# Second-layer weight blocks decoded at other beats, GpSimd tied to row maxima through pair 10, and other beats for two preparation steps

## The chip, the cores and the metric

The kernel runs on one core of a Trainium2 chip. The metric is device time in microseconds (us), the median of several runs. The core's engines each take their own instructions in order: TensorE (PE, matmuls into PSUM), VectorE (DVE), ScalarE (ACT) and GpSimd (POOL). SyncE (SP) issues most DMAs.

## The reference

Eight batches of 12 heads, 448 rows, head size 64, all in float32. Queries and keys are normalised by their root mean square and a gain, softmax attention follows, and its output feeds a layer that takes the largest of three products.

```python
q_n, k_n = (rmsnorm(q, g_q), rmsnorm(k, g_k))
scores = scale * np.matmul(q_n, k_n.transpose(0, 1, 3, 2))
scores = scores - np.max(scores, axis=-1, keepdims=True)
attn = np.exp(scores)
attn = attn / (np.sum(attn, axis=-1, keepdims=True) + 1e-09)
attn_out = np.matmul(attn, v)
x = attn_out.transpose(0, 2, 1, 3).reshape(B * S, H * D)       # 3584 x 768
h = np.maximum(np.maximum(x @ w1, x @ w2), x @ w3)
out = h @ w_out
```

## The kernel before

**Pairs, chunks, beats.** Two heads of a batch make a pair g; there are 48 pairs, six to a batch. The 448 query rows of a pair go in four chunks c = 0 to 3, the last half as large. The whole order of work is written out by hand: the function `beat(g, i)` is called for each pair with i = 0 to 11, and every engine gets its instructions in the order in which the beats emit them. A counter `clock` counts beats (12 g + i), and `later(n, work)` emits work at the end of the beat n beats on. Chunk (g, c) below is chunk c of pair g.

**One chunk.** PE multiplies queries and keys into a PSUM tile `sc` (`scores`, L680, and L687 for the short chunk) at beat 12 g + 3 c - 1. There are two such tiles, so the scores of a chunk can start only when the chunk two earlier has let its tile go. DVE reads the tile for the row maximum (`row_max`, L702), from chunk (6, 1) on at the beat 12 g + 3 c, ACT takes the exponential (L718), DVE adds a small number to the sums and inverts them (L798, L802), ACT writes the upper float16 half of the weights `pp` (L805), and DVE writes the lower half from `sc` and `pp` (`lower_weights`, L815). That last instruction, one for each head, lets `sc` go; it is emitted right behind the row maximum of the next chunk. SP transposes `pp` by DMA (L828, L834) into `pt`, and PE multiplies it with the values (L860). The first six pairs (`PLAIN`) do this in float32 and transpose on PE (L738, copied out by ACT at L751).

**Preparing a pair.** Two pairs ahead, GpSimd squares the rows (L450), DVE sums them (L457), GpSimd forms the inverse root (L467, L471) and scales keys and queries (L479, L488). ACT writes their upper halves (L499), GpSimd the lower halves `kp` and `qp` (L505), and SP transposes both (L519) and swaps the keys' halves (L526). The values of a pair are scaled on GpSimd (L633), and split by ACT (L641) and GpSimd (L647). For the first three batches a bound on the values is found with products on PE (`largest_v`, L593: twelve matmuls into a PSUM tile `marks`) that DVE reduces (L169, `v_rows`); for later ones DVE reduces the values itself, in two parts.

**Weights.** The weights come as 24 blocks of 128 by 768, 18 of the first layer and six of the second, and each is decoded once. `prep_block(n)` has ACT rescale it (L189) and DVE run three steps on it, one to three beats apart (L197, L201, L206, 128x768 words each, SBUF to SBUF). A second-layer block is then multiplied with itself on PE (L260, six matmuls into `marks`, seven beats on) and reduced by DVE (L169, `o_row`, nine beats on). First-layer blocks are scaled and split in threes by ACT (L310) and DVE (L313). When the sixth second-layer block is decoded, `bound_out` starts ten beats on, and ACT (L365) and DVE (L370) split the six. `load_raw` brings the next raw block, by SP.

**The layer's matmuls.** `ffn` makes a queue of them for a batch, layer 1 (L889) and layer 2 (L951), and `thirds` lets some two groups of three out in each beat, between the attention's instructions. The queue opens at beat 78. All PSUM tiles but `sc` and the attention's output share one ring of three (`ps_m`): `acc` of the layer, `marks`, `most`, `turned`. What takes a tile of the ring waits until the tile three before it has been read.

**The tie.** `follow` (L164, L165) puts a 1x1 memset on DVE and a 1x1 copy of it on GpSimd, so that GpSimd goes on only when DVE has come that far. It stands ahead of every row maximum up to chunk (6, 0), and nowhere later. The lines that set the beats of the second-layer blocks are

```python
n_in = min(decoded[0], NFT * NJ)
due_at = BLOCK_BEATS[0] * n_in + BLOCK_BEATS[1] * (decoded[0] - n_in)
if decoded[0] < len(blocks) and clock[0] > due_at:
    later(0, lambda n=decoded[0]: prep_block(n), True)
```

with `BLOCK_BEATS = (4, 8)`: first-layer blocks at beats 1, 5, ... 69, second-layer blocks at 73, 81, 89, 97, 105, 113.

Of the kernel before, what the change touches and what calls it, by code (L numbers as in the profile page):

```python
# [32 lines left out]
SQUARE = 1.0 + 2.0 ** -5  # L33


BLOCK_BEATS = (4, 8)


PLAIN = 6


LOADS = 14
# [6 lines left out]
def qknorm_attention_maxout_ffn_kernel(  # L49
# [43 lines left out]
    NFT = DF // P  # L93
# [1000 lines left out]
    def beat(g, i):  # L1094
# [6 lines left out]
        if part == 0:  # L1101
            if g < G:
                if k > 4 * PLAIN:
                    row_max(g, c)
                softmax(g, c)
            if early:
                scores(*divmod(k + 1, 4))
            if g < PLAIN:
                if c > 0:
                    turn_plain(g, c - 1)  # L1110
            elif k == 4 * PLAIN:
                pass
            elif 0 < k <= 4 * G:
                lower_weights(*divmod(k - 1, 4))
# [32 lines left out]
        if g + 1 < G:  # L1147
            if g + 1 < PLAIN:
                if i in (1, 4):
                    turn_whole(g + 1, "kq"[i // 4])  # L1150
                if i in (2, 5):
                    keep_whole(g + 1, "kq"[i // 5])
            else:
                if i == 0:
                    upper_rows(g + 1, "q")
                if i in (0, 1):
                    lower_rows(g + 1, "kq"[i])
                if i in (2, 3):
                    turn_rows(g + 1, "kq"[i - 2])
                if i == 5:  # L1160
                    swap_keys(g + 1)

# [15 lines left out]
        elif n < G:  # L1178
            if i in (0, 3):
                squares(n, "kq"[i // 3])  # L1180
            if i in (2, 5):
                sum_squares(n, "kq"[i // 3])
            if i in (5, 7):
                inv_rms(n, "kq"[i // 7])
            if i in (8, 9):
                scale_rows(n, "kq"[i - 8])

        if g == 0 and i in (0, 3):
            load_v(i // 3)
            later(10 if i == 0 else 11, lambda: largest_v(i // 3))  # L1190
        if g % 3 == 0 and g + 6 < G and i == 9:
            load_v(g // 3 + 2)
            later(8, lambda: largest_v(g // 3 + 2))
        if g == 1 and i == 4:
            bound_v(0)
        if g % NP == NP - 1 and g + 1 < G and i == 7:
# [16 lines left out]
            turn_weights(w, 3)  # L1213
        if PLAIN <= g < G and i in (5, 8, 11):
            turn_weights(g, i // 3 - 1)
        n_in = min(decoded[0], NFT * NJ)
        due_at = BLOCK_BEATS[0] * n_in + BLOCK_BEATS[1] * (decoded[0] - n_in)
        if decoded[0] < len(blocks) and clock[0] > due_at:
            later(0, lambda n=decoded[0]: prep_block(n), True)
            decoded[0] += 1  # L1220
        tick()
# [41 lines left out]
```

## Time and profile before

| what | us |
|---|---|
| median of 3 runs | 1016.45 |
| range of the runs | 1015.76 to 1019.43 |
| the profiled execution's own time | 1017.41 |
| its span in the trace | 1015.6 |
| PE busy | 977.4 |
| DVE busy | 692.9 |
| ACT busy | 624.7 |
| GpSimd busy | 602.4 |

The span leaves 1.8 us outside the trace. A timeline row gives start, duration, engine, line, operation and tiles, and in brackets the idle time before it and what ended it. A row of windows gives for a stretch its length, the busy time of PE, PE's weight loads (PEld), DVE, ACT and GpSimd with the count of instructions, the granted PE clock as a share of full speed, the DMA engines' share and GB/s. "PE is busy" means that a matmul is in flight.

In the trace before, beat 73 lies near 111 us, beat 80 (scores of chunk (6, 3)) at 127.4, beat 83 (scores of (7, 0)) at 133.9 and beat 95 (scores of (8, 0)) at 158.3.

### The profile page before, as it was taken

The numbers are of one execution on the slowest core, as the hardware profiler recorded it, in microseconds if no ns is written. First come the engines' busy times: TensorE is split into PE (matmuls) and PEld (weight loads), VectorE is DVE, ScalarE is ACT, GpSimd is POOL, SyncE is SP. The second block draws the span as 40 slices with busy tenths as digits, with TensorE's granted clock in tenths as the row PEclk, the third lists the DMA queues.
The fourth block names the chain that finished last, engine by engine and source line by source line (L and its number), as shares of the span: only waits on it lengthen the run. The fifth ranks groups of instructions, "written<-read, shape, count | busy, mean of one in ns | idle before, by whom it ended". The sixth has DMA issues, their size and how long they took to land.

```text
span 1015.6 us, 17562 instructions
## 1 busy us (share of the span) xinstructions
PE 977.4 (96%) x6045; PEld 527.5 (52%) x6045; DVE 692.9 (68%) x1365; ACT 624.7 (62%) x1419; POOL 602.4 (59%) x683
## 2 busy tenths in 40 slices
PE   8988689889999999999999999999999999999998
PEld 5555345445555555555555555555555555555554
DVE  6899988887767666685767666775767657660120
ACT  6798675667666765666666666657666766651111
POOL 6677875678566666666776666666667757310000
PEclk9999889999999999999999999999999999999999
DMA  9867798989999899998989999999989998751001
GB/s 241 226 174 188 197 179 177 186 149 163 209 165 179 165 204 183 186 166 172 204 155 184 174 206 166 190 159 190 197 162 182 176 186 139 146 92 55 1 1 63
DMA packets 519550, 165.95 MB, mean 163 GB/s; under 512 B 494436, under 2 KB 515236, under 8 KB 519460
## 3 DMA queue, kind: packets, MB, share of 16 engines
q1 hardware_dynamic: 456480, 148.83, 75.5%
q10 hardware_dynamic: 62980, 16.00, 8.6%
q8 instruction: 48, 0.79, 0.3%
q14 instruction: 42, 0.34, 0.1%
HBM read 53.28 MB, written 11.01 MB: 63 GB/s over the span
## 4 chain that ended last, share of the span: by engine, by line
PE 60%; DMA 1%; DVE 0%; ACT 0%; issue 0%; SPq 0%
PE acc L889 34%; PE acc L951 12%; PE av L860 6%; PE sc L680 6%; PE sc L687 1%; DMA pt<-pp 0%; DVE pp L815 0%; DMA out_dram<-osb 0%; ACT osb L960 0%; DVE nm L702 0%; ACT pp L805 0%; ACT qp L499 0%; PE most L604 0%; ACT ht L909 0%; SPq L834 0%
## 5 line engine op out<-in xcount | busy, mean ns | idle before, releaser
L889 PE MATMUL acc<-xt,w_sb 128*128 128x448 f16 x2592 | 516.4, 354 | 0.0
L889 PEld LDWEIGHTS <-w_sb 128*128 128x128 f16 x2592 | 251.4, 98 | 242.3 <-issue 14.0
L718 ACT ACTIVATE sc<-sc,nm 128x448 f32<-128x448 f32 x294 | 178.9, 609 | 187.5 <-DVE nm L702 182.9
L702 DVE TENSOR_REDUCE nm<-sc 128x2 f32<-128x896 f32 x192 | 186.2, 970 | 99.4 <-PE sc L680 58.5
L805 ACT ACTIVATE pp<-sc,rs 128x448 f16<-128x448 f32 x294 | 173.0, 633 | 80.3 <-ACT sc L718 36.4
L815 DVE SCALAR_TENSOR_TENSOR pp<-sc,rs,pp 128x448 f16<-128x448 f32 x294 | 187.9, 675 | 0.9 <-ACT pp L805 0.9
L471 POOL TENSOR_TENSOR ri<-ri,half_neg 128x7 f32<-128x7 f32 x96 | 146.6, 1527 | 8.0
L951 PE MATMUL acc<-w_sb,ht 128*128 128x384 f16 x864 | 148.1, 326 | 1.6 <-ACT osb L960 1.3
L505 POOL TENSOR_TENSOR kp<-kn,kp 128x448 f16<-128x448 f32 x42 | 43.5, 1036 | 157.9 <-ACT kp L499 142.3
L680 PE MATMUL sc<-kt,qt 128*128 128x448 f16 x504 | 116.8, 354 | 10.6 <-DVE pp L815 10.4
L951 PEld LDWEIGHTS <-ht 128*128 128x128 f16 x864 | 83.7, 98 | 61.0 <-issue 5.8
L680 PEld LDWEIGHTS <-qt 128*128 128x128 f16 x504 | 48.8, 98 | 56.4 <-DVE pp L815 10.7
L860 PE MATMUL av<-pt,vp 128*64 128x448 f16 x672 | 72.6, 355 | 0.6 <-DMA pt<-pp 0.6
L918 POOL COPY hx<-ht 128x128 f16<-128x128 f16 x48 | 15.4, 322 | 95.6 <-DVE ht L913 94.9
L875 DVE SCALAR_TENSOR_TENSOR xt<-av,xt 128x448 f16<-128x448 f32 x42 | 26.2, 624 | 62.6 <-ACT xt L874 62.6
L647 POOL TENSOR_TENSOR vp<-vr,vp 128x512 f16<-128x512 f32 x42 | 49.3, 1174 | 21.0 <-ACT vp L641 21.0
L457 DVE TENSOR_REDUCE ss<-sq 128x7 f32<-128x448 f32 x96 | 57.9, 603 | 5.1 <-ACT sq L448 4.3
L505 POOL TENSOR_TENSOR qp<-qn,qp 128x448 f16<-128x448 f32 x42 | 46.3, 1103 | 22.3 <-ACT qp L499 21.4
L903 DVE TENSOR_TENSOR m<-acc,m 128x448 f32<-128x448 f32 x54 | 33.1, 614 | 33.1 <-PE acc L889 33.0
L860 PEld LDWEIGHTS <-vp 128*64 128x64 f16 x672 | 36.0, 109 | 34.7 <-issue 15.8
L488 POOL TENSOR_TENSOR qn<-qn,gain 128x448 f32<-128x448 f32 x42 | 49.0, 1167 | 3.3
L467 POOL TENSOR_SCALAR ri<-ss 128x7 f32<-128x7 f32 x54 | 20.1, 373 | 51.1 <-DVE ss L457 49.9
(140 smaller groups left out, 1159.2 us busy)
## 6 DMA issues: line engine op xcount, KB each, us to landing
raw<-in_moe_w_dram SPq DMA_DIRECT2D x18, 768.0 KB, 5.6
kt<-kt SPq DMA_DIRECT2D x84, 112.0 KB, 2.6
out_dram<-osb SPq DMA_DIRECT2D x24, 384.0 KB, 2.6
vr<-in_v_dram SPq DMA_DIRECT2D x42, 192.0 KB, 4.2
kr<-in_k_dram ACTq DMA_DIRECT2D x34, 224.0 KB, 3.1
qr<-in_q_dram ACTq DMA_DIRECT2D x34, 224.0 KB, 4.4
raw<-in_moe_w_out_dram SPq DMA_DIRECT2D x6, 768.0 KB, 5.0
vs<-vp SPq DMA_DIRECT2D x84, 48.0 KB, 2.5
```

The source lines that it names most:

```text
L457: nc.vector.tensor_reduce(sums[g % 2][:, KQ[what]], sq, axis=AX, op=ALU.add)
L471: nc.gpsimd.tensor_tensor(out=ri, in0=ri, in1=half_neg[:, at], op=ALU.pow)
L505: nc.gpsimd.tensor_tensor(out=parts[:, :, 1], in0=n, in1=parts[:, :, 0], op=ALU.subtract)
L647: nc.gpsimd.tensor_tensor(out=vp[:, 1], in0=values_of(g).rearrange("p h n d -> p (h n) d"), in1=vp[:, 0], op=ALU.subtract,)
L680: nc.tensor.matmul(sc[:, h, :S], qt[:, 4 * h + c], kt[:, n, keys[h]], start=n == 0, stop=n == 1,)
L702: nc.vector.tensor_reduce(nm[:, :n], sc[:, :n, :S], axis=AX, op=ALU.max, negate=True)
L718: nc.scalar.activation(to, sc[:, h, :S], AF.Exp, bias=nm[:, h:h + 1], accum_out=total,)
L805: nc.scalar.activation(pp[:, h, 0], sc[:, h, :S], AF.Copy, scale=rs[:, h:h + 1])
L815: nc.vector.scalar_tensor_tensor(out=pp[:, h, 1], in0=sc[:, h, :S], scalar=rs[:, h:h + 1], in1=pp[:, h, 0], op0=ALU.mult, op1=ALU.subtract,)
L860: nc.tensor.matmul(av[half, :S], values, pt[:, 7 * h + block, SHIFT[h]:SHIFT[h] + S], start=n == 0, stop=n == len(steps) - 1,)
L889: nc.tensor.matmul(acc[:, :S], wt[:, wp, c], xs[c][:, xp], start=(c == 0 and n == 0), stop=(c == NCT - 1 and n == 2),)
L951: nc.tensor.matmul(acc[:, :HW], lhs, wo_sb[:, f, wp, half * HW:(half + 1) * HW], start=(f == 0 and n == 0), stop=(f == NFT - 1 and n == 2),)
```

## The change

1. Second-layer blocks are decoded at beats 79, 86, 91, 98, 103, 110. First-layer blocks keep their beats.
2. Pairs 6 to 10: a `follow` ahead of the row maximum of chunks 0, 1 and 3 (not of (6, 0), which has one), 14 in all.
3. In beats of pairs 6 to 10 the lower half of the next pair's queries moves from i = 1 to i = 3, their transposing DMA from i = 3 to i = 4. The scaling of the keys two pairs ahead moves from i = 8 to i = 9.
4. `largest_v` from the third value tile on comes 11 beats behind its load, not 8: three beats later, in every third pair.

```diff
-BLOCK_BEATS = (4, 8)
+BLOCK_BEATS = tuple(range(0, 72, 4)) + (78, 85, 90, 97, 102, 109)
...
+TIED = 11
...
                 if k > 4 * PLAIN:
+                    if g < TIED and c != 2:
+                        follow()
                     row_max(g, c)
...
-                if i in (0, 1):
-                    lower_rows(g + 1, "kq"[i])
-                if i in (2, 3):
-                    turn_rows(g + 1, "kq"[i - 2])
+                if i in (0, 3 if PLAIN <= g < TIED else 1):
+                    lower_rows(g + 1, "kq"[i > 0])
+                if i in (2, 4 if PLAIN <= g < TIED else 3):
+                    turn_rows(g + 1, "kq"[i > 2])
...
-            if i in (8, 9):
-                scale_rows(n, "kq"[i - 8])
+            if i == (9 if g < TIED else 8):
+                scale_rows(n, "k")
+            if i == 9:
+                scale_rows(n, "q")
...
-            later(8, lambda: largest_v(g // 3 + 2))
+            later(11, lambda: largest_v(g // 3 + 2))
...
-        n_in = min(decoded[0], NFT * NJ)
-        due_at = BLOCK_BEATS[0] * n_in + BLOCK_BEATS[1] * (decoded[0] - n_in)
-        if decoded[0] < len(blocks) and clock[0] > due_at:
+        if decoded[0] < len(blocks) and clock[0] > BLOCK_BEATS[decoded[0]]:
             later(0, lambda n=decoded[0]: prep_block(n), True)
```

What it moves on the engines is shown at three places; in the rows of the change a line number is up to five higher than before, since the file has grown (L702 is L705, L197, L201, L206 are L200, L204, L209, L815 is L818, L165 is L168).

DVE from the row maximum of chunk (6, 1), before:

```order
L702 TENSOR_REDUCE nm<-sc 128x2
L815 SCALAR_TENSOR_TENSOR pp<-sc,rs,pp 128x448 x2
L197 TENSOR_SCALAR w_sb<-raw 128x768
L798 TENSOR_SCALAR rs<-sc 128x2
L802 RECIPROCAL rs<-rs 128x2
L617 TENSOR_SCALAR v_down<-v_most 128x1
L621 RECIPROCAL v_up<-v_down 128x1
L201 SCALAR_TENSOR_TENSOR w_sb<-raw,w_sb 128x768
L313 SCALAR_TENSOR_TENSOR w_sb<-w_sb,w_up 128x768
L457 TENSOR_REDUCE ss_129<-sq 128x7
L206 SCALAR_TENSOR_TENSOR w_sb<-raw,w_sb 128x768
L702 TENSOR_REDUCE nm<-sc 128x2
```

and with the change:

```order
L705 TENSOR_REDUCE nm<-sc 128x2
L818 SCALAR_TENSOR_TENSOR pp<-sc,rs,pp 128x448 x2
L801 TENSOR_SCALAR rs<-sc 128x2
L805 RECIPROCAL rs<-rs 128x2
L620 TENSOR_SCALAR v_down<-v_most 128x1
L624 RECIPROCAL v_up<-v_down 128x1
L316 SCALAR_TENSOR_TENSOR w_sb<-w_sb,w_up 128x768
L460 TENSOR_REDUCE ss_129<-sq 128x7
L705 TENSOR_REDUCE nm<-sc 128x2
```

The three decode steps of the first second-layer block are gone from between these two row maxima; they now stand behind the row maximum of (6, 3).

GpSimd in pair 6, from the lower half of the queries to the values' scaling, before (`qp` the lower half of queries, `kn` and `qn` scaled keys and queries, `vr` values):

```order
L505 TENSOR_TENSOR qp<-qn,qp 128x7x64
L613 TENSOR_TENSOR v_most<-v_most,root 128x1
L450 TENSOR_TENSOR sq<-qr 128x448
L467 TENSOR_SCALAR ri<-ss_129,k_mean,k_eps 128x7
L471 TENSOR_TENSOR ri<-ri,half_neg 128x7
L467 TENSOR_SCALAR ri<-ss_129 128x7
L471 TENSOR_TENSOR ri<-ri,half_neg 128x7
L479 TENSOR_TENSOR kn<-kr,ri 128x448
L479 TENSOR_TENSOR qn<-qr,ri 128x448
L488 TENSOR_TENSOR qn<-qn,gain 128x448
L633 TENSOR_SCALAR vr<-vr,v_up 128x512
```

and with the change:

```order
L168 COPY seen<-here 1x1
L508 TENSOR_TENSOR qp<-qn,qp 128x7x64
L453 TENSOR_TENSOR sq<-qr 128x448
L470 TENSOR_SCALAR ri<-ss_129,k_mean,k_eps 128x7
L474 TENSOR_TENSOR ri<-ri,half_neg 128x7
L470 TENSOR_SCALAR ri<-ss_129 128x7
L474 TENSOR_TENSOR ri<-ri,half_neg 128x7
L168 COPY seen<-here 1x1
L482 TENSOR_TENSOR kn<-kr,ri 128x448
L482 TENSOR_TENSOR qn<-qr,ri 128x448
L491 TENSOR_TENSOR qn<-qn,gain 128x448
L636 TENSOR_SCALAR vr<-vr,v_up 128x512
```

Each `seen` copy holds what stands behind it until DVE has reached a row maximum: the first that of (6, 1), the second that of (6, 3).

DVE from the row maximum of (7, 2), where the values' `marks` are reduced, before:

```order
L702 TENSOR_REDUCE nm<-sc 128x2
L815 SCALAR_TENSOR_TENSOR pp<-sc,rs,pp 128x448 x2
L169 TENSOR_REDUCE o_row<-marks 128x1
L903 TENSOR_TENSOR m<-acc,m 128x448
L169 TENSOR_REDUCE v_rows<-marks 128x1
```

and with the change, from the memset ahead of the row maximum of (7, 3):

```order
L167 MEMSET here 1x1
L705 TENSOR_REDUCE nm<-sc 128x1
L818 SCALAR_TENSOR_TENSOR pp<-sc,rs,pp 128x448 x2
L172 TENSOR_REDUCE v_rows<-marks 128x1
L200 TENSOR_SCALAR w_sb<-raw 128x768
L801 TENSOR_SCALAR rs<-sc 128x1
L805 RECIPROCAL rs<-rs 128x1
L204 SCALAR_TENSOR_TENSOR w_sb<-raw,w_sb 128x768
L172 TENSOR_REDUCE o_row<-marks 128x1
```

The two `marks` no longer stand next to each other behind one row maximum; the decode steps of a second-layer block now follow the tied row maximum of the short chunk.

## The prediction

> **What bounds the kernel now.** The page's first part says that PE is nearly always busy.
>
> ```profile
> PE 977.4 (96%) x6045; PEld 527.5 (52%) x6045; DVE 692.9 (68%) x1365; ACT 624.7 (62%) x1419; POOL 602.4 (59%) x683
> ```
>
> So I asked next for the windows of a few stretches, to see where the other 38 us of the span lie.
>
> ```profile
> 110.00:160.00 50.00, 39.44 (x225) 21.25 (x226) 44.62 (x79) 31.62 (x68) 35.66 (x35) 0.83 0.85 185
> 160.00:250.00 90.00, 82.95 (x518) 43.51 (x515) 76.38 (x151) 63.32 (x139) 67.59 (x68) 1.00 0.90 165
> 250.00:950.00 700.00, 698.81 (x4240) 371.50 (x4239) 465.88 (x949) 433.54 (x1005) 420.94 (x479) 1.00 0.92 168
> ```
>
> From 250 to 950 us PE is idle for 1.2 of 700 us at full clock: that stretch is a queue of matmuls, and what an earlier stage gains or loses reaches the end unchanged. Between 110 and 250 us PE is idle for 10.6 + 7.0 us, DVE is busy for 89% and 85%, and the clock falls. All that the change moves lies there, but for three-beat shifts of `largest_v`. Third, PE's waits from 115 to 250 us (us in total, times, longest).
>
> ```profile
> PE sc L680 <- DVE pp L815: 9.8, 7, 3.0
> PE sc L687 <- DVE pp L815: 3.3, 1, 3.3
> PE marks L593 <- DVE o_row L169: 2.6, 1, 2.6
> PE acc L951 <- ACT osb L960: 1.3, 1, 1.3
> ```
>
> These, all but one of 0.3 us, sum to 17.0 us, and nearly all wait for DVE: scores wait for `lower_weights` (L815) to let their PSUM tile go. The timeline of PE shows where.
>
> ```profile
> 121.06 1.18 PE L680 MATMUL sc<-kt,qt 128*128 128x448 f16 x4 [3.04 <-DVE pp L815]
> 127.41 0.96 PE L687 MATMUL sc<-kt,qt 128*64 128x448 f16 x4 [3.27 <-DVE pp L815]
> ...
> 144.13 0.92 PE L680 MATMUL sc<-kt,qt 128*128 128x448 f16 x4 [1.39 <-DVE pp L815]
> ...
> 148.75 1.41 PE L593 MATMUL marks<-vr 128*128 128x128 bf16 x12 [2.56 <-DVE o_row L169]
> ...
> 182.70 0.93 PE L680 MATMUL sc<-kt,qt 128*128 128x448 f16 x4 [1.78 <-DVE pp L815]
> ...
> 188.19 0.93 PE L680 MATMUL sc<-kt,qt 128*128 128x448 f16 x4 [0.81 <-DVE pp L815]
> ```
>
> These are, in order, the scores of (6, 2), (6, 3), (7, 2), the products for a value tile, and the scores of (9, 1) and (9, 2). The rest, 17.0 less 12.85, is 4.15 us behind 200 us. So DVE's order in pairs 6 to 9 sets the time here, and only this can be won.
>
> **The change, part by part.** *(a) Pair 6.* DVE's timeline from the row maximum of (6, 1):
>
> ```profile
> 118.75 1.08 DVE L702 TENSOR_REDUCE nm<-sc 128x2 f32<-128x896 f32 x1
> 119.74 1.26 DVE L815 SCALAR_TENSOR_TENSOR pp<-sc,rs,pp 128x448 f16<-128x448 f32 x2
> 120.93 0.55 DVE L197 TENSOR_SCALAR w_sb<-raw 128x768 uint32<-128x768 uint32 x1
> 121.39 0.15 DVE L798 TENSOR_SCALAR rs<-sc 128x2 f32<-128x2 f32 x1
> ...
> 121.91 0.94 DVE L201 SCALAR_TENSOR_TENSOR w_sb<-raw,w_sb 128x768 uint32<-128x768 uint32 x1
> 122.76 1.01 DVE L313 SCALAR_TENSOR_TENSOR w_sb<-w_sb,w_up 128x768 f16<-128x768 f32 x1
> ...
> 124.22 0.95 DVE L206 SCALAR_TENSOR_TENSOR w_sb<-raw,w_sb 128x768 uint32<-128x768 uint32 x1
> 125.09 1.08 DVE L702 TENSOR_REDUCE nm<-sc 128x2 f32<-128x896 f32 x1
> 126.09 1.27 DVE L815 SCALAR_TENSOR_TENSOR pp<-sc,rs,pp 128x448 f16<-128x448 f32 x2
> ```
>
> The pair of L815 at 126.09 ends the 3.27 us wait. From start to next start the three decode steps take 0.46 + 0.85 + 0.87 = 2.2 us, all on that path, so (6, 3) starts 2.2 us earlier. The wait of (6, 2) ahead of it stays, since it ends with the L815 at 119.74 and nothing of the change stands before it. The three steps return behind the row maximum of (6, 3), ahead of that of (7, 0): 2.2 us more there. Against this, the L197 of the block at beat 81 and one `o_row` leave that place (0.46 and about 0.2 us), and so does a short idle time of DVE, which waited there for PE's scores:
>
> ```profile
> 134.87 1.09 DVE L702 TENSOR_REDUCE nm<-sc 128x2 f32<-128x896 f32 x1 [0.94 <-PE sc L680]
> ```
>
> With all of it, the row maximum of (7, 0) comes 2.2 - 2.2 + 0.66 + 0.94 = 1.6 us earlier. Bounds: 0 (the steps fully paid back) and 2.2.
>
> *(b) Pair 7,* from that row maximum to the one of (8, 0). Its windows, and the steps in it that lasted longer than their shortest:
>
> ```profile
> 134.87:159.69 24.82, 20.86 (x126) 10.93 (x125) 21.63 (x36) 14.29 (x32) 15.53 (x14) 0.93 0.90 192
> ```
> ```profile
> 136.47 1.37 DVE L313 SCALAR_TENSOR_TENSOR w_sb<-w_sb,w_up 128x768 f16<-128x768 f32 x1
> 137.75 1.90 DVE L201 SCALAR_TENSOR_TENSOR w_sb<-raw,w_sb 128x768 uint32<-128x768 uint32 x1
> 139.85 1.52 DVE L206 SCALAR_TENSOR_TENSOR w_sb<-raw,w_sb 128x768 uint32<-128x768 uint32 x1
> ...
> 150.67 0.94 DVE L197 TENSOR_SCALAR w_sb<-raw 128x768 uint32<-128x768 uint32 x1
> ```
> ```profile
> 138.81 1.74 POOL L505 TENSOR_TENSOR qp<-qn,qp 128x448 f16<-128x448 f32 x1
> ```
>
> The GpSimd instruction at 138.81 lies across the second and the third. The four steps took 0.36, 0.96, 0.57 and 0.39 us more than the 1.01, 0.94, 0.95 and 0.55 us of the rows under (a): 2.3 us. The tie starts GpSimd's work under a row maximum, which reads PSUM, and the row maxima here keep their 1.08 us. Of the six steps now in this pair (blocks 86 and 91) the first three follow an early tie whose GpSimd work is done by then, the last three stand right behind the tie of chunk 3; so I take half, 1.2 us. The wait of 2.56 us for `o_row` goes: the value tile's products come at beat 92, away from that reduction. So does the 1.39, or it is DVE's own time. What is late next is DVE itself: 21.63 busy, + 0.55 (six decode steps for five), - 1.2, and 1.0 of the pair's 3.2 us of idle time, which I let stay, is 22.0 us against 24.82: -2.8. Bounds: +0.6 (one step more and nothing else) and -4.9 (no step stretched, no idle time).
>
> [...]
>
> *(c) Pairs 8 and 9.* The block of beat 105 has its last two steps, L201 and L206, between the row maxima of (9, 0) and (9, 1), behind idle time in which DVE waits for ACT:
>
> ```profile
> 179.10 0.63 DVE L875 SCALAR_TENSOR_TENSOR xt<-av,xt 128x448 f16<-128x448 f32 x1 [2.17 <-ACT xt L874]
> ...
> 182.57 1.20 DVE L201 SCALAR_TENSOR_TENSOR w_sb<-raw,w_sb 128x768 uint32<-128x768 uint32 x1
> ```
>
> At beat 103 all three are done by (9, 0), two of them in that idle time. The 0.81 us wait goes, and 0.5 of the 1.78, whose other cause, ACT's late L805, is not touched: -1.3, between 0 and -2.6.
>
> *(d) Behind 200 us:* 4.15 us of waits, while `bound_out` and the six L370 come three beats earlier. The trace does not show that order. Between +1.5 (the size of the waits of a pair here, doubled) and -4.15 (all gone) I take a third of the gain, -1.4, since DVE is at 85% there, nearer to the busy pairs ahead than to 250 to 950 us with its 67%.
>
> *(e) Price of the ties.* The memset of a tie, by its line's own view (shortest, median and longest in ns):
>
> ```profile
> L164 DVE MEMSET here<- x24: 59/59/59, 14.0 to 111.3; 1x1 f32 x24
> ```
>
> Of 14 such memsets of 0.06 us, five stand in the pairs that DVE bounds: +0.3. GpSimd is busy for 15.53 of 24.82 us in pair 7, so it can wait for a row maximum. Behind the query transposes, one beat later on SP, stand the swap of keys and the first transposes of weights; ahead of them, before and now, stand the short chunk's transposes, which hide the beat. If they did not, the pair's first scores would be late by as much as `qp`. The raw loads stay ten beats ahead of their decoding or close to it. The later `largest_v` from pair 9 on costs nothing: DVE is idle for a third of 250 to 950 us and PE waits for nothing there.
>
> The sum is -1.6 - 2.8 - 1.3 - 1.4 + 0.3 = -6.8 us on the profiled execution's 1017.41 (span 1015.6 and 1.8 around it): 1010.6. The median of the runs is 0.96 lower, so I forecast 1009.6.
>
> **The rivals.** *More is won:* PE loses all waits but that of (6, 2), 17.0 less 3.04, or 14.0 us: 1017.41 - 14.0 - 0.96 = 1002.5. For it speaks the clock, which I gave nothing:
>
> ```profile
> 121.60:131.84 10.24, 6.97 (x37) 3.46 (x35) 9.81 (x18) 5.48 (x13) 7.86 (x7) 0.50 0.82 158
> ```
>
> Behind the 3.04 us wait PE ran at half clock, with 6.97 us of matmuls in it, so up to 3.5 us come back if the waits shorten. Against it: DVE is busy for 9.81 of these 10.24 us. [...]
>
> *Given back, no difference:* the decode steps of blocks 79, 91 and 103 stand just where the tie of chunk 3 starts GpSimd's longest run (`kn`, `qn`, gain, `vr`). If each step there is stretched like those above (0.39, 0.96 and 0.57), the two blocks in the pairs that DVE bounds lose 2 x 1.92 = 3.8 us: 1017.41 - 6.8 + 3.8 - 0.96 = 1013.4. For it speaks that GpSimd then starts first; against it, that L201 and L206 come one and two beats later.
>
> *Slower:* that run behind the tie of chunk 3 must end before ACT reads the values (L641). In pair 9 of before:
>
> ```profile
> 191.89 0.94 POOL L479 TENSOR_TENSOR kn<-kr,ri 128x448 f32<-128x448 f32 x1
> 192.79 1.34 POOL L479 TENSOR_TENSOR qn<-qr,ri 128x448 f32<-128x448 f32 x1
> 194.21 1.73 POOL L488 TENSOR_TENSOR qn<-qn,gain 128x448 f32<-128x448 f32 x1
> 195.92 0.69 POOL L633 TENSOR_SCALAR vr<-vr,v_up 128x512 f32<-128x512 f32 x1
> ```
> ```profile
> 194.87 0.61 DVE L702 TENSOR_REDUCE nm<-sc 128x1 f32<-128x448 f32 x1
> ```
> ```profile
> 199.81 0.63 ACT L641 CAST vp<-vr 128x512 f16<-128x512 f32 x1
> ```
>
> The run takes 4.7 us. Begun at 194.87 it ends at 199.6, 0.2 us ahead of its reader. Queued behind L641 on ACT is the next exponential, then the weights, and so PE's scores. If the run is stretched by another 1.5 us, ACT is 1.3 us late in each of five pairs, 6.5 us, and (a) to (c) are not won, since PE then waits for ACT: 1017.41 + 6.5 - 0.96 = 1023.0. The point from which it decides is a distance from row maximum to L641 below the run's length. Against it: `qn` is the same work as `kn` and took 0.40 us more, so this run is stretched already, and still ends in time.
>
> **How the numbers follow.** Forecast 0.54, more won 0.18, given back 0.20, slower 0.08. About 0.5%, 5.1 us, is what a measurement of this kernel can tell from no change. No change ends at 1011.4 and the forecast lies 1.8 us below, inside the bounds of (b) alone: of its 0.54 I give 0.04 to no change, and of the given-back case, 0.20, a tenth to faster. Faster 0.70, same 0.22, slower 0.08. The range runs from the best case, rounded down to 1002, over the given-back case to 1014.5 and leaves out the slower one and what lies beyond the ends.
>
> **What would show it.** Right: the wait of 3.27 us at (6, 3) down to about 1; no wait of `marks` for `o_row`; the row maxima of (7, 0) and (8, 0) about 1.6 and 4.4 us earlier; L201 and L206 of pair 7 near 0.95 us; fewer microseconds at clock 0.50. Wrong: steps of blocks 79 and 91 of over 1.5 us beside `qn` or its gain (given back), or ACT's L641 waiting for GpSimd's L633, with L718 late (slower), or PE waits moved to (8, 1) and (9, 1) of over 2 us.

## The result and the profile after

The changed kernel takes 1012.27 us, the median of 6 runs (1011.11 to 1013.04), beside 1017.66 us for the kernel before (6 runs, 1015.74 to 1019.43). The ratio is 0.9947, 95% interval 0.9932 to 0.9961, so 5.4 us or 0.53% are won, a little more than the 0.5% that can be told from no change. Run again beside other kernels it took 1011.37 us against 1016.30 (ratio 0.9957, 0.9944 to 0.9969); that is a little less than 0.5%, but both intervals leave out no change. The forecast of 1009.6 lies 2.7 us under the first median, which lies in its range of 1002 to 1014.5. All medians and ranges below are those of fast runs; one single execution of one kernel (no ties, `bound_out` later) took 2587.95 us and is left out.

The profiled execution of the changed kernel took 1013.04 us, with a span of 1011.3. The page's first part shows the busy times: PE was busy 3.3 us less than before, DVE as long as before.

```profile
PE 974.1 (96%) x6045; PEld 524.9 (52%) x6045; DVE 692.8 (69%) x1379; ACT 626.6 (62%) x1419; POOL 598.8 (59%) x697
```

The windows of the three stretches:

```profile
110.00:160.00 50.00, 39.41 (x228) 20.11 (x227) 44.68 (x85) 33.15 (x72) 36.63 (x43) 0.86 0.91 197
160.00:250.00 90.00, 85.09 (x545) 45.65 (x543) 76.84 (x162) 63.11 (x139) 66.63 (x77) 1.00 0.96 170
250.00:950.00 700.00, 698.48 (x4226) 370.33 (x4225) 464.14 (x944) 432.70 (x999) 416.33 (x474) 1.00 0.92 166
```

From 110 to 160 us PE idles for 10.6 us, as before, at a clock of 0.86 for 0.83; from 160 to 250 us it idles for 4.9 us and not 7.0; behind 250 us hardly anything changed (1.5 us idle for 1.2). PE's waits from 115 to 250 us:

```profile
PE sc L683 <- DVE pp L818: 7.0, 4, 3.1
PE marks L263 <- DVE v_rows L172: 3.3, 1, 3.3
PE sc L690 <- DVE pp L818: 2.1, 2, 1.6
PE marks L263 <- ACT m L902: 0.9, 1, 0.9
PE acc L954 <- ACT osb L963: 0.9, 1, 0.9
PE marks L284 <- DVE w_sb L209: 0.8, 1, 0.8
```

These, all but one of 0.2 us, sum to 15.0 us against 17.0. The waits for `lower_weights` fell from 13.1 to 9.1 us; the 2.6 us wait for `o_row` is gone, and a wait of 3.3 us for `v_rows` has come. PE's timeline shows where:

```profile
119.43 0.97 PE L683 MATMUL sc<-kt,qt 128*128 128x448 f16 x4 [3.12 <-DVE pp L818]
...
123.93 0.96 PE L690 MATMUL sc<-kt,qt 128*64 128x448 f16 x4 [1.64 <-DVE pp L818]
...
146.78 0.85 PE L596 MATMUL marks<-vr 128*128 128x128 bf16 x12
...
152.02 0.80 PE L263 MATMUL marks<-w_sb 128*128 128x128 bf16 x6 [3.25 <-DVE v_rows L172]
...
179.58 0.93 PE L683 MATMUL sc<-kt,qt 128*128 128x448 f16 x4 [0.84 <-DVE pp L818]
```

These are the scores of (6, 2), whose wait stays, and of (6, 3), whose wait is halved; the products of the fifth value tile; the products of the block decoded at beat 86, which need a tile of the ring of three and wait until the value tile's marks have been reduced; and the scores of (9, 1), with half of their wait. The waits at (7, 2) and (9, 2) are gone.

**Where the time came from.** The start of a chunk's row maximum (a row of L705, L702 before) marks how far the kernel is. For the changed kernel, the first chunks of pairs 6, 7 and 8 on DVE's timeline:

```profile
109.59 1.08 DVE L705 TENSOR_REDUCE nm<-sc 128x2 f32<-128x896 f32 x1
...
132.01 1.08 DVE L705 TENSOR_REDUCE nm<-sc 128x2 f32<-128x896 f32 x1
...
156.59 1.09 DVE L705 TENSOR_REDUCE nm<-sc 128x2 f32<-128x896 f32 x1 [0.68 <-PE sc L683]
```

So pair 6 lasted 132.01 - 109.59 = 22.42 us. The same is done for the other stretches and kernels in this table: the length before, and what each kernel's profiled execution adds to it or takes from it, in us (the kernels of the last four columns come below). "Second run" is the same changed kernel, run again beside others.

| from | to | before | change | change, second run | blocks alone | ties alone | values alone | no ties |
|---|---|---|---|---|---|---|---|---|
| (1, 0) | (3, 0) | 34.49 | -1.37 | -1.10 | -0.02 | -0.01 | -1.22 | -1.41 |
| (6, 0) | (7, 0) | 23.63 | -1.20 | -1.23 | -1.05 | +0.29 | -0.50 | -1.06 |
| (7, 0) | (8, 0) | 24.82 | -0.25 | -1.01 | -1.15 | -0.13 | -1.17 | +0.35 |
| (8, 0) | (10, 0) | 40.36 | -1.31 | -1.70 | -0.59 | +0.48 | -0.56 | -0.97 |
| (10, 0) | (11, 1) | 25.45 | +0.78 | +0.35 | +2.45 | -0.19 | -0.68 | +2.58 |
| (11, 1) | (12, 0) | 14.91 | -1.11 | -1.02 | -1.12 | 0.00 | 0.00 | -1.01 |

What is left, up to the last row maximum, is +0.1 for the change and -0.4 in its second run. A profile is one execution. The one of the kernel before took 1017.41 us, 1.1 to 1.3 above that kernel's medians beside the experiments, and the one of "values alone" (1013.90 us) is the fastest of its 12, so that column adds up to more than its median gives. Three of the entries were not in the forecast: 1.1 to 1.4 us are won in pairs 1 and 2, pair 7 gives little, and something is lost from pair 10 to 11 and won back behind it.

### The profile page after: what moved, and what is told of

It reads as the page before. It is cut to its first block, busy times and chain, and to the rows that moved or that the text cites. A ratio compares the mean times of both kernels' runs of the same rounds, so it can differ in the third digit from the quotient of the medians.

```text
span 1011.3 us, 17592 instructions
## 1 busy us (share of the span) xinstructions
PE 974.1 (96%) x6045; PEld 524.9 (52%) x6045; DVE 692.8 (69%) x1379; ACT 626.6 (62%) x1419; POOL 598.8 (59%) x697
## 4 chain that ended last, share of the span: by engine, by line
PE 60%; ACT 0%; DMA 0%; DVE 0%; issue 0%
PE acc L892 35%; PE acc L954 12%; PE av L863 6%; PE sc L683 6%; PE sc L690 1%; DMA out_dram<-osb 0%; DVE pp L818 0%; ACT osb L963 0%; DVE nm L705 0%; ACT pp L808 0%; ACT qp L502 0%; PE most L607 0%; ACT ht L912 0%; DVE ht L916 0%
## 5 line engine op out<-in xcount | busy, mean ns | idle before, releaser
L705 DVE TENSOR_REDUCE nm<-sc 128x2 f32<-128x896 f32 x192 | 186.5, 972 | 105.0 <-PE sc L683 61.9
L818 DVE SCALAR_TENSOR_TENSOR pp<-sc,rs,pp 128x448 f16<-128x448 f32 x294 | 188.1, 676 | 1.5 <-ACT pp L808 1.5
L921 POOL COPY hx<-ht 128x128 f16<-128x128 f16 x48 | 15.3, 318 | 94.5 <-DVE ht L916 93.6
L508 POOL TENSOR_TENSOR qp<-qn,qp 128x448 f16<-128x448 f32 x42 | 44.1, 1050 | 20.6 <-ACT qp L502 19.8
L801 DVE TENSOR_SCALAR rs<-sc 128x2 f32<-128x2 f32 (+1 forms) x168 | 26.1, 156 | 35.3 <-ACT sc L721 35.2
```

The source lines that it names most:

```text
L508: nc.gpsimd.tensor_tensor(out=parts[:, :, 1], in0=n, in1=parts[:, :, 0], op=ALU.subtract)
L705: nc.vector.tensor_reduce(nm[:, :n], sc[:, :n, :S], axis=AX, op=ALU.max, negate=True)
L818: nc.vector.scalar_tensor_tensor(out=pp[:, h, 1], in0=sc[:, h, :S], scalar=rs[:, h:h + 1], in1=pp[:, h, 0], op0=ALU.mult, op1=ALU.subtract,)
```

## The experiments

**Theories.** One: the decode beats make the gain. Two: the ties make it, by parting DVE's two-input steps from GpSimd. Three: the later value products make it. Later ones are told where they arise. The first four kernels take the change apart. Their medians, beside 1016.15 us for the kernel before (35 runs, 1014.83 to 1018.85):

| kernel | median us | runs from, to | ratio, 95% interval |
|---|---|---|---|
| blocks alone | 1016.12 | 1014.29, 1019.77 | 0.9999, 0.9989 to 1.0010 |
| ties alone | 1017.17 | 1015.60, 1018.08 | 1.0006, 0.9996 to 1.0016 |
| values alone | 1014.94 | 1013.90, 1016.68 | 0.9984, 0.9975 to 0.9994 |
| no ties | 1016.11 | 1013.18, 1017.72 | 0.9994, 0.9983 to 1.0004 |

**Blocks alone:** the change with

```diff
-TIED = 11
+TIED = PLAIN
-            later(11, lambda: largest_v(g // 3 + 2))
+            later(8, lambda: largest_v(g // 3 + 2))
```

> Only the beats of the second-layer blocks are new; no ties, old preparation beats, value products eight beats behind their load. If the decode beats make the gain (theory one): 4.5 to 6 us below the kernel before, the 3.27 us wait at (6, 3) down to about 1.6, row maximum of (6, 3) earlier by about 2 against (6, 0). If the ties make it by parting DVE's two-input steps from GpSimd (theory two): only 1 to 2 us below, and the steps of the blocks 79, 86 and 91 last 1.2 to 1.9 us again. If the later value products make it (theory three): 2 to 3 us below, since the 2.56 us wait for o_row then only changes its name. If the 1.65 us by which (6, 0) came earlier is variation between runs or the shift of largest_v in pairs 1 and 4, (6, 0) comes here within 0.5 us of the kernel before.

No difference is measured: the beats alone don't make the gain, and theory one falls. They do make nearly all of pair 6's (-1.05). And (6, 0) came only 0.25 us earlier, so what the change wins ahead of it belongs to the value products or to variation.

**Ties alone:** ties and shifted beats, with `BLOCK_BEATS` ending in 72, 80, 88, 96, 104, 112 and the products at 8.

> Ties of pairs 6 to 10 and the shifted preparation beats alone, blocks at their old beats, value products at eight beats. Theory one: no difference, between -1 and +1 us. Theory two: 3 us or more below the kernel before, with L201 and L206 of pair 7 near 0.95 us. Theory three: no difference. In all of them the 3.27 us wait at (6, 3) stays.

No difference. The ties are worth nothing with the blocks where they were: from (6, 0) to (10, 0) the second and third decode steps of the blocks even took 17.8 us together, against 16.4 before.

**Values alone:** the blocks as in ties alone, no ties, the products at 11.

> Only largest_v from the third value tile on is later, eleven beats behind its load. Theory one: 0 to 2 us below, as the 2.56 us wait for o_row goes but what DVE has queued is late next. Theory two: no difference. Theory three: 2.5 us or more below. If the shift in pairs 1 and 4 makes the 1.65 us ahead of (6, 0), the row maximum of (6, 0) comes 1.6 us earlier here; if it is variation between runs, within 0.5 us of the kernel before.

1.2 us below the median before, the only part that helps by itself. It does so in three places. One is pair 7, where the wait for `o_row` goes (-1.17), one lies from (10, 0) to (11, 1) (-0.68), where the sixth value tile's products stood ahead of the scores of (10, 3): DVE waited 2.42 us for these before and waits 1.93 us here. And one is pair 1, ahead of all that I had looked at. PE's timeline there, before:

```profile
35.78 0.86 PE L593 MATMUL marks<-vr 128*128 128x128 bf16 x12
36.57 0.97 PE L672 MATMUL sc<-kt,qt 64*64 64x448 f32 x4
37.47 1.08 PE L738 MATMUL turned<-ident,e 128*112 128x128 f32 x8
```

and with the later products alone (`marks` the value tile's products, `turned` a chunk's transposes):

```profile
35.68 0.92 PE L675 MATMUL sc<-kt,qt 64*64 64x448 f32 x4
36.53 1.08 PE L741 MATMUL turned<-ident,e 128*112 128x128 f32 x8
...
37.85 0.89 PE L596 MATMUL marks<-vr 128*128 128x128 bf16 x12
```

The third value tile's twelve matmuls stood ahead of a chunk's scores and of its transposes, which now come 0.9 us earlier (0.2 us of it was there at (1, 0)), and the chunks behind them with it.

**No ties:** the change with `TIED = PLAIN` only.

> The change without the ties and without the shifted preparation beats: blocks at their new beats, value products at eleven. Theory one: 5 to 6 us below the kernel before, as the whole change. Theory two: 1 to 2 us below, with stretched steps of blocks 79, 86 and 91. Theory three: 5 to 6 us below, most of it in pair 7. The wait of block 86's marks for v_rows, 3.25 us in the whole change, should be here as well, since the order on PE is the same.

No difference from the kernel before, so without ties the other two parts are worth nothing together, and with them 4 to 5 us. The table of stretches shows where to look: from (10, 0) to (11, 1) this kernel loses 2.58 us, the change 0.35 to 0.78. DVE's timeline without ties, between the row maxima of (10, 0) and (10, 1):

```profile
201.05 1.00 DVE L342 TENSOR_TENSOR o_block<-o_row,w_most 128x6 f32<-128x6 f32 x1 [0.52 <-POOL o_row L338]
...
202.15 1.24 DVE L916 SCALAR_TENSOR_TENSOR ht<-m,ht 128x448 f16<-128x448 f32 x1
203.32 1.08 DVE L705 TENSOR_REDUCE nm<-sc 128x2 f32<-128x896 f32 x1
```

and GpSimd's beside it:

```profile
200.98 1.04 POOL L508 TENSOR_TENSOR qp<-qn,qp 128x448 f16<-128x448 f32 x1
201.97 0.94 POOL L453 TENSOR_TENSOR sq<-qr 128x448 f32<-128x448 f32 x1
```

With the ties, in the changed kernel, the same steps of DVE and the tie of (10, 1) on GpSimd:

```profile
200.27 0.17 DVE L342 TENSOR_TENSOR o_block<-o_row,w_most 128x6 f32<-128x6 f32 x1 [0.52 <-POOL o_row L338]
...
200.99 0.62 DVE L916 SCALAR_TENSOR_TENSOR ht<-m,ht 128x448 f16<-128x448 f32 x1 [0.35 <-ACT ht L912]
201.54 1.09 DVE L705 TENSOR_REDUCE nm<-sc 128x2 f32<-128x896 f32 x1
```
```profile
201.75 0.17 POOL L168 COPY seen<-here 1x1 f32<-1x1 f32 x1 [1.51 <-DVE here L167]
201.89 1.02 POOL L508 TENSOR_TENSOR qp<-qn,qp 128x448 f16<-128x448 f32 x1
```

L342, six words wide, takes 1.00 us beside `qp` and 0.17 us alone; it ends at 202.05, as `qp` does at 202.02. The `ht` step behind it takes 1.24 us and not 0.62 beside `sq`. So the step of six words lasted until the end of the other instruction, here and in the later run of the shifted beats without ties (201.40 and 201.39 us). The tie holds `qp` behind the row maximum. These steps are `bound_out`'s, which starts ten beats behind the sixth block: at beat 120 and not at 123. So the new beats brought it beside GpSimd's lower half of the queries, and the tie, with the queries' lower half at its shifted beat, parts the two. By the row maxima that makes 0.7 us at (10, 1).

The loss does not end there. PE's scores of (10, 2) then wait for DVE for 2.52 us, and not 1.53, and behind the longer wait PE ran at half clock from 206 to 209.5 us (from 200 to 225 us its granted clock was 0.93, which is 3.5 us at 0.50):

```profile
205.63 1.12 PE L683 MATMUL sc<-kt,qt 128*128 128x448 f16 x4 [2.52 <-DVE pp L818]
206.55 3.97 PE L892 MATMUL acc<-xt,w_sb 128*128 128x448 f16 x12
```

The same twelve matmuls of the layer take 2.43 us in the change, where PE has its full clock there (1.00 from 200 to 225 us). In the blocks alone the wait is as long (2.53 us) and no half-clock stretch follows it (its granted clock from 160 to 250 us is 1.00).

**Theory four** is that places add up, with that collision taken away by the ties, and pair 7 given back to the wait for `v_rows`. A rival, theory five, is that small gains are lost in the clock, whose half-speed stretches fall differently in each run. The next four kernels stand beside 1016.30 us for the kernel before (26 runs, 1014.82 to 1019.95):

| kernel | median us | runs from, to | ratio, 95% interval |
|---|---|---|---|
| blocks and ties | 1013.71 | 1012.61, 1014.75 | 0.9977, 0.9968 to 0.9986 |
| only the third tile's products later | 1013.30 | 1011.83, 1013.73 | 0.9961, 0.9947 to 0.9974 |
| no ties, `bound_out` later | 1014.13 | 1013.48, 1016.29 | 0.9984, 0.9975 to 0.9993 |
| the change again | 1011.37 | 1010.45, 1012.00 | 0.9957, 0.9944 to 0.9969 |

**Blocks and ties:** the change with the products at 8.

> The whole change but for the value products, which stay eight beats behind their load. Theory four (places add up, and each part pays where the others leave room): pair 7 shorter by about 1.1 us, since no marks wait for v_rows and none for o_row; nothing won between (1, 0) and (3, 0), where the later products of the third tile gave 1.2 to 1.4 us; from (10, 0) to (11, 1) +0.8 and not +2.5, since the ties hold GpSimd off there; in all 3.5 to 4 us below the kernel before. Theory two in its strong form (ties pay in pairs 6 to 9): pair 7 shorter by 2 us or more. Rival five (the sums are lost in the clock's windows, which fall differently in each run): no difference from the blocks alone, 0 to 1 us below the kernel before.

2.6 us below the kernel before, and 2.4 below the blocks alone: ties pay with the new beats. The fifth theory's "no difference from the blocks alone" falls. Less was won than the 3.5 to 4 us that theory four gave: pair 7 gave 0.78 us and not 1.1, (10, 0) to (11, 1) lost 1.75 us and not 0.8, and the profiled execution lost 1.51 us from (3, 0) to (6, 0), where the kernel is the same as blocks alone (see the last section).

**Only the third tile's products later:**

```diff
-            later(11, lambda: largest_v(g // 3 + 2))
+            later(11 if g == 0 else 8, lambda: largest_v(g // 3 + 2))
```

> The whole change, with the products at eleven beats only for the third value tile (in pair 1) and at eight beats for the later ones. Theory four: both gains of the value products are kept and the wait of 3.25 us of block 86's marks for v_rows in pair 7 goes: pair 7 about 1.1 us shorter than before, (1, 0) to (3, 0) about 1.3 us shorter, in all 1 to 1.5 us below the whole change. Rival five: no difference from the whole change.

It is not below the whole change but 1.9 us above it by the medians (the intervals of the ratios overlap). Pair 7 (-0.80) is no shorter than in the change's second run, although the wait for `v_rows` is gone, and (10, 0) to (11, 1) lost 1.76 us again. PE's timeline of this kernel shows why the last:

```profile
207.16 0.89 PE L596 MATMUL marks<-vr 128*128 128x128 bf16 x12 [1.31 <-DVE o_up L352]
```

The sixth value tile's products, at eight beats, run into `bound_out`: their tile of the ring is held until L352 has read it. At eleven beats they don't. The same row, with the same 1.31 us, stands in the blocks alone. So in the profiles the three-beat shift pays for the third and the sixth tile; the medians can't tell the sixth from variation.

**No ties, `bound_out` later:** no ties, and

```diff
-            later(10, bound_out, True)
+            later(13, bound_out, True)
```

> The change without ties, with bound_out thirteen beats behind the sixth block instead of ten, that is at the beat where the kernel before has it. Theory four: the 2.5 us that blocks without ties lose from (10, 0) to (11, 1) go, and with them the 1.0 us won behind: about 1.5 us below the version without ties, so 2 us below the kernel before. If the loss there comes from anything else than the place of bound_out beside GpSimd's lower half of queries (rival: the earlier split of the six blocks), the 2.5 us stay.

As expected: 2.0 us below the version without ties, with -0.33 from (10, 0) to (11, 1) in place of +2.58, and +0.01 behind it in place of -1.01. The loss came with the place of `bound_out`.

**The change again:** the same kernel.

> The changed kernel once more, beside the others on one chip. Every theory but the fifth: 4 to 5.5 us below the kernel before. Rival five: between 0 and 3 us below, as the 5.4 us of the first six runs then were partly a matter of where the clock's windows fell.

4.9 us below by the medians, 4.4 by the ratio: theory five's 0 to 3 us are not met.

The last four ask what the waits and the ties are worth. The kernel before took 1016.25 us beside the first three (17 runs, 1014.65 to 1019.58) and 1016.30 beside the last (17 runs).

| kernel | median us | runs from, to | ratio, 95% interval |
|---|---|---|---|
| fifth tile's products at 14 | 1011.09 | 1009.82, 1011.72 | 0.9940, 0.9925 to 0.9955 |
| ties in pair 10 only | 1015.35 | 1011.89, 1016.49 | 0.9981, 0.9970 to 0.9993 |
| ties, `bound_out` later | 1011.82 | 1011.46, 1012.41 | 0.9951, 0.9937 to 0.9965 |
| shifted beats without ties | 1015.93 | 1014.39, 1018.15 | 0.9991, 0.9981 to 1.0001 |

**Fifth tile's products at 14:**

```diff
-            later(11, lambda: largest_v(g // 3 + 2))
+            later(14 if g == 6 else 11, lambda: largest_v(g // 3 + 2))
```

> The whole change, with the products of the fifth value tile three beats later again, fourteen beats behind its load, so that they stand behind the scores of (8, 0) and block 86's marks no longer wait 3.25 us for v_rows in pair 7. If PE's wait there is the price (theory six): 2 to 3 us below the whole change, pair 7 shorter by 2 us or more than in it. If DVE and ACT set the end of pair 7 and the wait on PE only shows where PE is early (theory four, as the products at eight beats put a wait of 2.5 us for ACT's exponential in its place): 0 to 1 us below the whole change, with a wait of PE for ACT L721 or DVE at the scores of (8, 0) or (8, 1).

0.28 us below the change's second run, which is no difference, though the wait of 3.25 us is gone. PE's timeline of this kernel shows what stands in its place:

```profile
152.31 0.92 PE L683 MATMUL sc<-kt,qt 128*128 128x448 f16 x4 [2.31 <-ACT sc L721]
```

and its row of windows for pair 7, with DVE's three pieces of idle time in it, shows what sets the end:

```profile
132.46:156.29 23.83, 18.38 (x123) 9.41 (x122) 20.71 (x41) 15.72 (x33) 15.58 (x19) 1.00 0.86 171
```
```profile
135.97 0.62 DVE L460 TENSOR_REDUCE ss<-sq 128x7 f32<-128x448 f32 x1 [0.55 <-POOL sq L453]
...
140.00 0.16 DVE L801 TENSOR_SCALAR rs<-sc 128x2 f32<-128x2 f32 x1 [0.69 <-ACT sc L721]
...
148.93 0.63 DVE L916 SCALAR_TENSOR_TENSOR ht<-m,ht 128x448 f16<-128x448 f32 x1 [1.74 <-ACT ht L912]
...
156.29 1.08 DVE L705 TENSOR_REDUCE nm<-sc 128x2 f32<-128x896 f32 x1
```

DVE is busy for 20.71 of 23.83 us and idles 0.55 + 0.69 + 1.74 = 2.98 us for GpSimd and ACT; from 148.93 on it works without a break up to the row maximum of (8, 0), which no longer waits for PE (0.68 us in the change). In the change's second run PE waits the same 3.25 us and the row maximum of (8, 0) doesn't wait at all. So that wait was slack but for the 0.68 of one execution: theory six falls, theory four holds here. This kernel has the lowest median of all, but can't be told from the change.

**Ties in pair 10 only:** `g == 10` in place of `g < TIED` and of `PLAIN <= g < TIED`, in the ties and the shifted beats.

> The whole change, but the ties and the shifted preparation beats only in pair 10, not in pairs 6 to 9: three ties in place of fourteen. If the ties pay by holding GpSimd off bound_out's steps in pair 10 (theory four): within 1 us of the whole change, L342 of 0.17 us and not 1.00, and L916 of 0.62 us and not 1.24, between the row maxima of (10, 0) and (10, 1); (10, 0) to (11, 1) +0.4 to +0.8 against the kernel before. If they pay in pairs 6 to 9 (theory two): like the version without ties, 3 to 4 us above the whole change.

Here theory four's claim that the ties pay only in pair 10 fell. The steps in pair 10 are as expected (L342 0.17 us, L916 0.63, and +0.13 from (10, 0) to (11, 1)), yet the median is 4.0 us above the change's second run, as theory two has it. So the ties, with the beats that were shifted for them, pay in pairs 6 to 9 too. How is only partly shown. From (6, 0) to (10, 0) this kernel's profile won 2.3 us, the change's second run 3.9. It is not the sum of the decode steps; L209's and L204's groups from 112 to 200 us (count, busy us, mean ns), first of the version without ties:

```profile
L209 DVE SCALAR_TENSOR_TENSOR w_sb<-raw,w_sb 128x768 uint32<-128x768 uint32 x7 | 8.9, 1266 | 0.0
L204 DVE SCALAR_TENSOR_TENSOR w_sb<-raw,w_sb 128x768 uint32<-128x768 uint32 x7 | 6.6, 945 | 0.0
```

and of the change's second run:

```profile
L209 DVE SCALAR_TENSOR_TENSOR w_sb<-raw,w_sb 128x768 uint32<-128x768 uint32 x7 | 7.7, 1100 | 0.0
L204 DVE SCALAR_TENSOR_TENSOR w_sb<-raw,w_sb 128x768 uint32<-128x768 uint32 x7 | 7.6, 1092 | 0.0
```

15.5 us against 15.3: the ties move the stretch from one step to the other. Where it falls matters. Without ties, GpSimd scales `qn` beside the last decode step of block 86 in pair 7, here in this kernel:

```profile
145.53 1.62 DVE L209 SCALAR_TENSOR_TENSOR w_sb<-raw,w_sb 128x768 uint32<-128x768 uint32 x1
```

In the change this step takes 0.95 us (at 145.52), and the stretch falls on an L204 behind the row maximum of (7, 3) (1.62 us at 152.68). The L209 stands ahead of the reciprocals of (7, 2), for which ACT's weights wait; behind these stands ACT's part of `ht`, for which DVE's L916 waits. So without the tie L916 comes at 149.16 us and not at 148.49, and the row maximum of (7, 3) at 150.63 and not at 149.97. The reduction of the value tile behind it is late by as much, PE waits for it for 3.92 us and not 3.25, and the row maximum of (8, 0) waits 0.67 us for PE. The same holds in every profile with the new beats: the L209 takes 1.43 to 1.62 us in the five without ties there and 0.95 in the six with them, and counted from (6, 0) the row maximum of (7, 3) comes 2.6 to 2.7 us earlier than before in the five and 3.2 to 3.5 in the six. The row maximum of (8, 0) waits 0.5 to 1.2 us for PE in the four without ties that have the products at eleven beats, and not at all in the six with ties but for the change's first profile (0.68). From (6, 0) to (10, 0) the five took 86.0 to 87.1 us, five of the six 84.7 to 84.9, and the change's first profile 86.0.

The profiled execution of this kernel was one of its fastest (1013.09 us, second of 12). The runs say more than the profile: with ties through pairs 6 to 10 and the new beats they lie within 2.2 us of each other in each of the five kernels of these experiments that have both (5 to 11 runs each), and without ties in pairs 6 to 9 within 2.8 to 5.5 us (six kernels, 10 to 12 runs each). The granted clock does not sort this kernel's runs (1011.89 us at a mean clock of 0.989, 1015.94 us at 0.992). What the longer runs contain no profile here shows, and where the rest of the 4.0 us lies stays open.

**Ties, `bound_out` later:** the change with `bound_out` at 13.

> The whole change, ties kept, with bound_out thirteen beats behind the sixth block, where the kernel before has it. If ties and the later bound_out are two ways past the same collision (theory four): no difference from the whole change, within 0.7 us, the -1.0 from (11, 1) to (12, 0) gone and about as much won from (10, 0) to (11, 1). If each pays by itself (rival): 1.5 to 2 us below the whole change.

0.45 us above the change's second run, no difference: -0.11 from (10, 0) to (11, 1), +0.01 behind it. With the ties a later `bound_out` wins nothing that can be told; the rival's further 1.5 to 2 us fall.

**Shifted beats without ties:** the change with the `follow()` of pairs 6 to 10 taken out, all else kept.

> The whole change with all 14 new ties left out, but with the preparation beats that the change shifts in pairs 6 to 10 (lower half of the queries, their transposing DMA, scaling of the keys) kept at their new places. If holding GpSimd back is what pays (theory seven): like the version without ties and shifts, 1014.5 to 1016.5 us, with over 2.5 us between its fastest and its slowest run, L342 of about 1.0 us and the step behind it stretched. If the shifted beats alone part the steps (rival): like the whole change, 1011 to 1012.5 us, with runs within 2 us of each other.

Like the version without ties: 1015.93 us, runs 3.8 us apart, +2.59 from (10, 0) to (11, 1), L342 0.99 us and L916 1.24. So the shifted beats alone pay nothing. That the ties would pay without them is not shown: no run has that, and it is the shift to i = 3 that puts `qp` behind the tie of chunk 1.

## Why the prediction was right or wrong

The sum was -6.8 us; -5.4 was measured, and in the second run -4.9 by the medians (-4.4 by the ratio). Its terms fit less well than their sum, and that the sum came this near is in part luck: 1.1 to 1.4 us in pairs 1 and 2, which the forecast put at nothing, stand in for what pair 7 and the stretches behind (10, 0) did not give.

| term | forecast | change | second run |
|---|---|---|---|
| (a) pair 6 | -1.6 | -1.20 | -1.23 |
| (b) pair 7 | -2.8 | -0.25 | -1.01 |
| (c) pairs 8 and 9 | -1.3 | -1.31 | -1.70 |
| (d) behind (10, 0) | -1.4 | 0.0 | -0.8 |
| third tile's products | 0 | -1.37 | -1.10 |

(The term behind (10, 0) is the last two stretches of the table above and what comes behind them, from (12, 0) to (24, 0) and on to the last chunk: 0.78 - 1.11 + 0.93 - 0.57, and 0.35 - 1.02 + 0.58 - 0.66. Behind (12, 0) nothing is changed but the later `largest_v`, and the profiles of all these kernels lie there between -0.7 and +1.3 us in a stretch.)

**(a) was right,** mechanism and nearly size: the wait at (6, 3) went from 3.27 to 1.64 us (1.12 in the second run), its row maximum came 2.55 us earlier against (6, 0), where 2.2 were forecast, and about half of that was paid back by (7, 0). The blocks alone show -1.05.

**(b) failed in one step:** "1.0 of the pair's 3.2 us of idle time, which I let stay". DVE's busy time came as forecast (20.98 worked out, 20.78 and 20.71 measured), but the idle time did not shrink: the forecast kept 1.0 us of it, and 3.8 and 3.1 us were there. Before, DVE's idle time in pair 7 ended so:

```profile
150.20 0.29 DVE L169 TENSOR_REDUCE v_rows<-marks 128x1 f32<-128x128 f32 x1 [0.97 <-PE marks L593]
...
152.50 0.62 DVE L913 SCALAR_TENSOR_TENSOR ht<-m,ht 128x448 f16<-128x448 f32 x1 [0.88 <-ACT ht L909]
...
159.15 0.62 DVE L875 SCALAR_TENSOR_TENSOR xt<-av,xt 128x448 f16<-128x448 f32 x1 [1.18 <-ACT xt L874]
```

PE is gone from these releasers, but the rows shown above for the products at 14 have 3.0 us again, for GpSimd and ACT: DVE comes to its steps sooner and finds their inputs not yet there. Part of the 1.74 us for ACT is DVE's own order: ACT's weights wait for reciprocals that stand behind a decode step, as the L209 above shows. I took idle time as won where the next releaser stood just behind. That the wait for `o_row` returns as one for `v_rows` was missed as well, since I looked for the next reader of one reduction and not for the next user of the ring; it cost at most the 0.68 us for which DVE waited for PE in one of the two executions.

**(c) was right:** the wait at (9, 2) is gone and that at (9, 1) went from 1.78 to 0.84 us. From (9, 0) to (10, 0) the blocks alone give -1.0 us and the change -1.3; what pair 8 adds differs from kernel to kernel.

**(d) failed** in "while `bound_out` and the six L370 come three beats earlier", priced by a share of the waits and not by what stands beside it at the new beat. With the blocks alone that costs 2.5 us; with the ties, 0.4 to 0.8, and 1.0 to 1.1 come back one pair later.

**(e) was mis-sized by its sign.** I booked the ties as a price of 0.3 us and half of pair 7's stretch. The blocks' beats take most of that stretch away without them, and the ties' own worth is 2.4 us (blocks and ties against blocks alone) to 4.7 us (the change against no ties). Of these the profiles show about 2 us from (10, 0) to (11, 1) and, but for the change's first profile, 1.1 to 2.4 us from (6, 0) to (10, 0). By the medians ties in pair 10 only are worth less than that, 0.8 us against no ties, so the account is not closed.

**The missing term** is the third tile's products. "All that the change moves lies there, but for three-beat shifts of `largest_v`" put them aside, and "costs nothing" was argued for pair 9 on only. In pair 1 they stood in front of a chunk's scores and transposes.

**The rivals.** *Given back:* the place was right, the size small. In the changed kernel, a step of block 79, one of block 86 and one of block 91:

```profile
130.75 1.33 DVE L209 SCALAR_TENSOR_TENSOR w_sb<-raw,w_sb 128x768 uint32<-128x768 uint32 x1
...
141.94 0.95 DVE L204 SCALAR_TENSOR_TENSOR w_sb<-raw,w_sb 128x768 uint32<-128x768 uint32 x1
...
152.68 1.62 DVE L204 SCALAR_TENSOR_TENSOR w_sb<-raw,w_sb 128x768 uint32<-128x768 uint32 x1
```

The first and the last met GpSimd's run behind the tie of chunk 3: 0.38 and 0.67 us over 0.95, not 3.8 in all; the one between them, which was 1.90 us for the block then in pair 7, is not stretched. The sign named for this rival, a step of over 1.5 us beside `qn` or its gain, did come, once: the 1.62 us. *Slower:* did not come. In the changed kernel GpSimd's run ends with the values at 154.86, and ACT takes them at 155.51 with no wait:

```profile
153.48 1.38 POOL L636 TENSOR_SCALAR vr<-vr,v_up 128x512 f32<-128x512 f32 x1
```
```profile
155.51 0.64 ACT L644 CAST vp<-vr 128x512 f16<-128x512 f32 x1
```

The margin there is 0.65 us; in pair 6 it is only 0.03 (the values end at 131.28, ACT takes them at 131.31), so this rival was nearer than the forecast had it. *More won:* not reached; (6, 2) kept its 3.1 us wait as said, and half-clock stretches remained, though fewer of them: two with 13.6 us from 110 to 160 us, where there were three with 17.1. That the clock comes back when a wait gets shorter is not shown: behind waits of 2.52 us (no ties) and 2.53 us (blocks alone) PE ran once at half clock and once not.

## What to carry to other kernels

When a piece of work is moved to other beats, price everything that is timed from it (here `bound_out`, ten beats behind) by what stands beside it at the new place. A wait that goes is worth only the distance to the next releaser on the engine that sets the stage's end: PE's 3.25 us was worth at most 0.7. Parts of a change can be worth nothing one by one and 5 us together, so a tie, which holds one engine back, is to be tried with the order that it is meant to protect. A step that is stretched costs by what waits behind it: here 0.67 us more on a decode step ahead of the reciprocals made ACT, the next row maximum and then PE late.

## What the runs showed of the hardware

Two executions of the same changed kernel had their half-clock stretches at different places, as the windows around them show, first of the change, then of its second run:

```profile
120.20:127.02 6.82, 5.18 (x27) 2.52 (x27) 6.42 (x14) 5.32 (x11) 3.23 (x5) 0.50 0.99 194
...
150.92:157.74 6.82, 5.72 (x20) 2.65 (x20) 6.10 (x13) 3.70 (x9) 5.86 (x8) 0.50 0.82 189
```
```profile
119.20:122.62 3.42, 2.94 (x16) 1.59 (x16) 3.09 (x8) 1.82 (x4) 2.70 (x5) 0.50 1.07 277
...
153.34:156.75 3.41, 3.41 (x11) 1.36 (x10) 3.41 (x6) 3.03 (x6) 2.53 (x5) 0.50 1.04 208
```

The instructions and PE's 3.25 us wait in pair 7 were the same, yet once 6.82 us at half clock began inside that wait and once 3.41 us began 1.1 us behind it, and pair 7 differed by 0.76 us. The four stretches last 3.41 us or twice that, and the two of an execution start a whole multiple of it apart (30.72 us, nine times, and 34.14 us, ten times), while from one execution to the other the first starts 1.00 us apart. So the instructions, which are the same in both, don't alone set where they fall. A stretch of one profile can differ by more than 0.76 us: blocks alone and blocks and ties give the same instructions up to pair 6, yet from (3, 0) to (6, 0) the second took 1.51 us more; from 57.5 to 67.5 us its granted clock was 0.66, against 1.00 in the first (over the whole executions 0.991 against 0.995). So a difference of that size in one stretch of two profiles is not read by itself, unless, as at (7, 3), it returns in every profile. The medians decide.

A DVE step of six words per partition (L342) took 0.83 us longer beside a GpSimd instruction of 1.04 us (1.00 and not 0.17 us), and one of 768 words 0.67 us longer (L209, 1.62 and not 0.95 us).
